# A new order for attention and two feed-forward layers on one core: one pair of blocks after the other, two batches later, sums on VectorE

## The chip, the cores and the metric

The kernel runs on one core of one Trainium2 chip. The core has TensorE (PE, matmul; its weight loads are shown apart as PEld), VectorE (DVE), ScalarE (ACT), GpSimd (POOL) and SyncE (SP), which here issues the DMA transfers. The metric is the device time of one execution in microseconds (us), as the median of the runs.

## The reference

```python
def _attn_ref(q, k, v, g_norm):            # (4 batches, 8 heads, 576, 64), float32
    kv = np.einsum('bhsd,bhse->bhde', k, v)
    out = np.einsum('bhsd,bhde->bhse', q, kv)
    rms = np.sqrt(np.mean(out * out, axis=-1, keepdims=True) + 1e-06)
    return (out / rms * g_norm).astype(np.float32)

def _moe_ref(x, w_a, w_b, w_out):          # x (2304, 512); d_ff 1536
    a = x @ w_a
    b = x @ w_b
    return (a * b @ w_out).astype(np.float32)

def _moe2_ref(x, w_in, w_out):             # d_ff 2048
    h = x @ w_in
    g = np.maximum(h, 0.0) + np.log1p(np.exp(-np.abs(h)))
    return (g @ w_out).astype(np.float32)
```

The output of the attention, heads side by side, goes through the first layer and then the second. The weights are 64-bit floats.

## The kernel before

**Numbers.** A float32 operand is split into two fp32r halves, hi (ACT) and lo (DVE: value minus hi), and a product is made of three fp32r matmuls, hi·hi, hi·lo, lo·hi. A native float32 matmul needs no split. Each weight is loaded raw (64 bits, 512 KB a tile) and turned into float32 by two ACT and one DVE operation (`w_load`, `w_start`, `w_value`), then split (`w_split`: one ACT, one DVE operation).

**Tiles.** The 2304 tokens are five blocks: four of 512 (block j is the first 512 tokens of batch j - 1), and block 0 with the 64 left of each batch. Blocks (1, 2) are pair 0, (3, 4) pair 1. For most of the work the two blocks of a pair and the two halves of the model dimension make a 2 x 2 matrix, which is multiplied in seven products instead of eight: A11, A12, A22 take blocks as they are, S1 to S4 sums of them. `x_sums` (L877) makes these sums and splits for the first layer, 14 operand tiles of 512 KB a pair; `w_sums` (L746) makes the matching sums of the weights, four DVE operations of half width for two tiles.

**Stages, as recorded.** `attention(b)` (L1311) computes a batch: kv by small matmuls, `att_o` for q times kv, the norm, the split into x. Batch 0 (NATIVE_O) copies kv (`kv_copy`) and multiplies in native float32; batches 1 to 3 split kv (`kv_half`) and q (`halves`) and use three matmuls. `slots(j)` (L1380) is the first layer for F0 = 4 of the 12 chunks of d_ff for block j of pair 0, in plain products; these chunks are fp 0 and 1 (an fp is two chunks). The other fps of pair 0 and all of pair 1 are jobs `take(n)` (L1417) in the order of ORDER: weights of the fp for both matrices, then `gated` (L909), seven products for each of a and b; for pair 1 also `first0`, block 0. A weight comes from `job_first` (L822) at first use, which also makes its sums; where the second use doesn't follow at once, it stores the float32 tiles to DRAM (`drop`), and `job_again` (L851) loads and splits them anew. `job_out` (L862) prepares w_out. After the last job of a pair `second1(pair)` (L1002) multiplies by w_out. While ORDER mixes the pairs (`x_place`, L1409), `hold` stores the 14 operand tiles of each pair to DRAM, and `take` fetches those of its pair where they are not in SBUF. `job_keep` (L757) prepares the weights of the second layer. That layer: `op_steps(pair)`, then for eight pieces a pair `stage1(i)` (L1103), seven products and softplus, and `g_sums(i)` (L1138), two sums of 128x512 on POOL, and behind the eight pieces `stage2_2(pair)` (L1162), whose operands are split from these pieces and sums; block 0 goes with pair 1 (`single1`, `single2`).

**Order and buffers.** The calls are recorded as steps (up to six matmuls into one tile are one step), and PLAN, a permutation of the steps written out by a planner, is the order in which they are emitted (`emit`, L292). Every engine and SP's queue works in that order. SBUF holds 39 big tiles of 512 KB, 28 of 256 KB, and PSUM 8 banks; a step takes a free buffer when it is emitted and waits until its last user is done. `among(main, *others)` (L1296) records the steps of others evenly between those of main. The calls around the change:

```python
    among(slots(1), attention(1))
    among(slots(2), attention(2))
    x_sums(0)
    # ...
    among(take(0), attention(3))
    x_sums(1)
```

All operations carry the line of a helper, L296, so the groups are told apart by the names of their tiles: op halves of operands, w halves of weights, w1o and w2o the output weights fetched for second1 and stage2_2, kept_* tensors in DRAM.

Of the kernel before, what the change touches and what calls it, by code (L numbers as in the profile page):

```python
# [13 lines left out]
ALU = mybir.AluOpType  # L14
# [20 lines left out]
F0 = 4  # L35
# [13 lines left out]
ORDER = ((0, 2), (1, 2), (0, 3), (0, 4), (0, 5), (1, 3), (1, 4), (1, 5), (1, 0), (1, 1))  # L49


# [4 lines left out]
NATIVE_O = (0,)  # L56
# [266 lines left out]
def attention_gated_softplus_kernel(  # L323
# [14 lines left out]
    nc = Record(tc.nc)  # L338
# [483 lines left out]
    def job_first(m, fp):  # L822
# [14 lines left out]
        for k, x in enumerate(l):  # L837
            w_load(x)
            w_start(x)
            w_value(x)  # L840
            made(k, x, 0)
        w_sums(l, True)
        for k, x in enumerate(l):
            if not plain:
                made(2 + k, x, 1)
# [712 lines left out]
```

## Time and profile before

| | us |
|---|---|
| median of 3 runs (896.19 to 897.7) | 896.82 |
| the profiled execution | 895.69 |
| its span, first to last instruction | 893.9 |
| PE busy, 4084 matmuls | 831.6 (93%) |
| PE weight loads | 676.2 (76%) |
| DVE busy, 1088 | 640.0 (72%) |
| ACT busy, 911 | 497.2 (56%) |
| POOL busy, 40 | 50.8 (6%) |
| DMA | 247.72 MB, mean 277 GB/s |

Busy time is the union of an engine's instructions, so overlapped ones count once, and a mean duration can be longer than what one more instruction costs. A wait is put down to what came last.

### The profile page before, as it was taken

The numbers are of one execution on the slowest core, as the hardware profiler recorded it, in microseconds if no ns is written. First come the engines' busy times: TensorE is split into PE (matmuls) and PEld (weight loads), VectorE is DVE, ScalarE is ACT, GpSimd is POOL, SyncE is SP. The second block draws the span as 40 slices with busy tenths as digits, with TensorE's granted clock in tenths as the row PEclk, the third lists the DMA queues.
The fourth block names the chain that finished last, engine by engine and source line by source line (L and its number), as shares of the span: only waits on it lengthen the run. The fifth ranks groups of instructions, "written<-read, shape, count | busy, mean of one in ns | idle before, by whom it ended". The sixth has DMA issues, their size and how long they took to land. (4 is left out here: it accounts for less than half of the span.)

```text
span 893.9 us, 11820 instructions
## 1 busy us (share of the span) xinstructions
PE 831.6 (93%) x4084; PEld 676.2 (76%) x4084; DVE 640.0 (72%) x1088; ACT 497.2 (56%) x911; POOL 50.8 (6%) x40
## 2 busy tenths in 40 slices
PE   7798999989989999999989999978999999988997
PEld 4576878868767887777778877757878878876785
DVE  2787999889978486888976956878763523378761
ACT  4786899867744656677646633565542211446430
POOL 0000000000000000000000000162000000090000
PEclk9998999999999999999999999998999999999999
DMA  9997799998989849988979799985679560563643
GB/s 261 324 311 272 292 320 354 401 375 324 327 280 395 328 159 334 337 299 310 334 256 385 284 408 337 327 283 177 213 244 396 182 253 22 190 209 116 195 146 124
DMA packets 109003, 247.72 MB, mean 277 GB/s; under 512 B 9616, under 2 KB 58768, under 8 KB 108944
## 3 DMA queue, kind: packets, MB, share of 16 engines
q1 hardware_dynamic: 108800, 246.98, 78.4%
q8 instruction: 32, 0.52, 0.2%
q14 instruction: 27, 0.22, 0.1%
q10 hardware_dynamic: 144, 0.00, 0.0%
HBM read 170.92 MB, written 76.02 MB: 276 GB/s over the span
## 5 line engine op out<-in xcount | busy, mean ns | idle before, releaser
L296 PE MATMUL acc<-op,w2o 128*128 128x512 f32 x672 | 161.4, 397 | 15.5 <-DVE op L296 12.1
L296 PEld LDWEIGHTS acc<-op,w2o 128*128 128x128 f32 x672 | 127.2, 191 | 46.4 <-DVE op L296 14.6
L296 DVE TENSOR_TENSOR w<-raw,w 128x512 fp32r<-128x512 f32 x168 | 113.8, 696 | 31.7 <-ACT w L296 30.8
L296 ACT ACTIVATE w<-raw 128x512 fp32r<-128x512 f32 x168 | 107.6, 669 | 48.2 <-DVE raw L296 10.3
L296 DVE TENSOR_TENSOR op<-g,op 128x512 fp32r<-128x512 f32 x156 | 110.8, 744 | 27.9 <-ACT op L296 27.7
L296 ACT ACTIVATE op<-g 128x512 fp32r<-128x512 f32 x156 | 90.9, 622 | 68.5 <-DVE g L296 36.9
L296 ACT ACTIVATE raw<-raw 128x512 int32<-128x512 uint8 (+1 forms) x136 | 88.5, 674 | 45.0 <-DMA raw<-in_w_out 30.9
L296 PE MATMUL acc<-op,w1o 128*128 128x512 f32 x420 | 100.9, 393 | 9.3 <-DMA w1o<-kept_wo 6.0
L296 PEld LDWEIGHTS acc<-op,w1o 128*128 128x128 f32 x420 | 77.2, 188 | 28.9 <-DMA w1o<-kept_wo 7.8
L296 DVE SCALAR_TENSOR_TENSOR raw<-raw 128x512 int32<-128x512 int32 x74 | 50.2, 686 | 10.3 <-ACT raw L296 10.1
L296 POOL TENSOR_TENSOR s<-g 128x512 f32<-128x512 f32 x14 | 21.2, 1520 | 581.3 <-ACT g L296 581.3
L296 PE MATMUL x<-op,w 128*128 128x512 f32 x192 | 48.5, 391 | 2.2 <-DMA w<-kept 2.2
L296 PE MATMUL v<-op,w 128*128 128x512 f32 x192 | 48.7, 391 | 0.8 <-DMA w<-kept 0.8
L296 PE MATMUL z<-op,w 128*128 128x512 f32 x192 | 48.3, 390 | 0.8 <-DMA w<-kept 0.8
L296 PEld LDWEIGHTS x<-op,w 128*128 128x128 f32 x192 | 35.6, 188 | 10.5 <-issue 1.9
L296 DVE TENSOR_TENSOR c<-z,p 128x512 f32<-128x512 f32 x32 | 21.9, 686 | 29.2 <-PE z L296 29.2
L296 PEld LDWEIGHTS z<-op,w 128*128 128x128 f32 x192 | 35.6, 188 | 8.4 <-DMA w<-kept 1.3
L296 PEld LDWEIGHTS v<-op,w 128*128 128x128 f32 x192 | 35.6, 188 | 8.4 <-DMA w<-kept 1.2
L296 PEld LDWEIGHTS h<-x,w 128*128 128x128 f32 x288 | 38.0, 191 | 5.0 <-ACT sb L296 1.5
L296 PE MATMUL h<-x,w 128*128 128x256 f32 x288 | 39.2, 283 | 1.7 <-ACT sb L296 1.1
L296 DVE TENSOR_TENSOR raw<-raw,raw 128x256 f32<-128x256 f32 x82 | 33.3, 418 | 0.4
L296 ACT ACTIVATE g<-x 128x512 f32<-128x512 f32 x16 | 9.5, 591 | 42.8 <-PE x L296 31.2
(143 smaller groups left out, 1437.3 us busy)
## 6 DMA issues: line engine op xcount, KB each, us to landing
w<-kept SPq DMA_DIRECT2D x80, 512.0 KB, 6.9
kept<-w SPq DMA_DIRECT2D x64, 512.0 KB, 6.1
w2o<-kept SPq DMA_DIRECT2D x112, 256.0 KB, 5.1
raw<-in_w_out SPq DMA_DIRECT2D x28, 512.0 KB, 6.6
w1o<-kept_ws SPq DMA_DIRECT2D x40, 256.0 KB, 6.1
kvraw<-in_kv SPq DMA_DIRECT2D x19, 448.0 KB, 9.7
kept_x_S<-op SPq DMA_DIRECT2D x16, 512.0 KB, 7.2
op<-kept_x_S SPq DMA_DIRECT2D x16, 512.0 KB, 8.4
```

The source lines that it names most:

```text
L296: f(*(x.place() if isinstance(x, View) else x for x in args), **{k: x.place() if isinstance(x, View) else x for k, x in kwargs.items()},)
```

## The change

ORDER lists the four jobs of pair 0 first and then the six of pair 1. `x_place` is then false for both pairs, so nothing is held. `attention(2)` is recorded among job 2, which is (0, 4), `attention(3)` among job 3, (0, 5). `x_sums(1)` comes behind `second1(0)`. NATIVE_O holds all four batches, with two kvf tiles in turn. The sums of the weights of fp 0 and 1 are made when they are loaded again, not at first use. `g_sums` runs on VectorE. PLAN is another permutation, of 3482 steps where there were 3534, made with transfer times taken from a trace.

```diff
-ORDER = ((0, 2), (1, 2), (0, 3), (0, 4), (0, 5), (1, 3), (1, 4), (1, 5), (1, 0), (1, 1))
+ORDER = ((0,2),(0,3),(0,4),(0,5),(1,0),(1,1),(1,2),(1,3),(1,4),(1,5))
+BATCHES_AT = {2: [2], 3: [3]}
-NATIVE_O = (0,)
+NATIVE_O = (0,1,2,3)
 PLAN = """
...
@@ job_first
-        w_sums(l, True)
+        if not plain:
+            w_sums(l, True)
@@ job_again
+        if 2 * fp < F0:
+            w_sums([(("f", m, fp, k),) for k in range(2)], True)
@@ g_sums
-        nc.gpsimd.tensor_tensor(out=t, in0=a21, in1=a22, op=ALU.add)
-        nc.gpsimd.tensor_tensor(out=a21, in0=a11, in1=a21, op=ALU.subtract)
+        nc.vector.tensor_tensor(out=t, in0=a21, in1=a22, op=ALU.add)
+        nc.vector.tensor_tensor(out=a21, in0=a11, in1=a21, op=ALU.subtract)
...
+    def run_all(steps):
+        for f in steps:
+            f()
...
     among(slots(1), attention(1))
-    among(slots(2), attention(2))
+    run_all(slots(2))
...
-    among(take(0), attention(3))
-    x_sums(1)
-    if x_place(1) or ORDER[1][0] == 0:
+    run_all(take(0))
+    if x_place(1):
+        x_sums(1)
         hold(1, True)
...
+        if n in BATCHES_AT:
+            l += [f for b in BATCHES_AT[n] for f in attention(b)]
         among(take(n), l)
         done.append(ORDER[n])
         if ORDER[n] == max(x for x in ORDER if x[0] == 0):
...
-            run(second1(0))
+            if -1 in BATCHES_AT:
+                among(drawn(second1(0), 64), [f for b in BATCHES_AT[-1] for f in attention(b)])
+            else:
+                run(second1(0))
+            x_sums(1)
```

## Rows read from the trace of the kernel before

**Rows 1.** The page: span, then busy us (share of span) and instructions of each engine.

```profile
span 893.9 us, 11820 instructions
PE 831.6 (93%) x4084; PEld 676.2 (76%) x4084; DVE 640.0 (72%) x1088; ACT 497.2 (56%) x911; POOL 50.8 (6%) x40
```

**Rows 2.** Stretches: start:end, length, busy PE, PEld, DVE, ACT, POOL (instructions), PE clock, DMA share, GB/s.

```profile
28.00:290.00 262.00, 243.20 (x1265) 195.82 (x1264) 230.55 (x421) 194.58 (x366) 0.00 (x0) 0.97 0.93 332
290.00:584.00 294.00, 279.84 (x1377) 231.59 (x1376) 222.38 (x391) 172.40 (x312) 6.89 (x5) 1.00 0.86 315
584.00:893.90 309.90, 285.47 (x1309) 234.36 (x1307) 175.38 (x252) 114.40 (x205) 42.25 (x28) 0.98 0.57 195
28.00:76.00 48.00, 39.87 (x244) 31.23 (x242) 37.16 (x70) 35.89 (x69) 0.00 (x0) 0.92 0.99 316
76.00:165.00 89.00, 88.28 (x507) 71.57 (x506) 83.34 (x153) 79.38 (x156) 0.00 (x0) 0.98 0.90 320
584.00:615.00 31.00, 22.86 (x82) 17.00 (x81) 26.49 (x29) 18.52 (x35) 18.41 (x12) 0.89 0.75 255
665.00:785.00 120.00, 118.03 (x598) 100.28 (x597) 46.51 (x73) 31.75 (x57) 2.90 (x3) 1.00 0.57 206
785.00:815.00 30.00, 25.01 (x113) 19.93 (x112) 25.57 (x27) 13.32 (x26) 20.94 (x14) 1.00 0.68 220
887.50:893.90 6.40, 0.00 (x0) 0.00 (x0) 0.65 (x1) 0.00 (x0) 0.00 (x0) 0.80 0.80 297
```

**Rows 3.** Waits of PE: tile, releaser, us in total, times, longest us.

```profile
PE acc L296 <- DVE op L296: 12.4, 7, 3.6
PE acc L296 <- DMA w1o<-kept_wo: 6.0, 3, 3.0
PE kvps L296 <- DMA kvraw<-in_kv: 4.8, 5, 2.5
PE kvps L296 <- DVE z L296: 4.7, 1, 4.7
```

**Rows 4.** Groups of POOL: tiles, shape, count, busy us, mean ns, idle before.

```profile
L296 POOL TENSOR_TENSOR g<-g,g 128x512 f32<-128x512 f32 x16 | 25.8, 1627 | 0.6
L296 POOL TENSOR_TENSOR s<-g 128x512 f32<-128x512 f32 x14 | 21.2, 1520 | 581.3 <-ACT g L296 581.3
```

**Rows 5.** Groups of DVE: two of 785 to 815 us, then two of the whole run.

```profile
L296 DVE TENSOR_TENSOR op<-g,op 128x512 fp32r<-128x512 f32 x10 | 12.1, 1237 | 0.5 <-ACT op L296 0.5
L296 DVE TENSOR_TENSOR out<-acc,out 128x512 f32<-128x512 f32 x4 | 2.7, 683 | 0.7 <-PE acc L296 0.7
...
L296 DVE TENSOR_TENSOR op<-g,op 128x512 fp32r<-128x512 f32 x156 | 110.8, 744 | 27.9 <-ACT op L296 27.7
L296 DVE TENSOR_TENSOR g<-s,g 128x512 f32<-128x512 f32 x26 | 23.2, 915 | 0.2
```

**Rows 6.** DVE in order of time: start, us, tiles, count of a run.

```profile
612.37 3.69 DVE L296 TENSOR_TENSOR op<-g,op 128x512 fp32r<-128x512 f32 x6
```

**Rows 7.** DMA issues: tiles, count, KB each, median us to landing.

```profile
kept_x_S<-op SPq DMA_DIRECT2D x16, 512.0 KB, 7.2
...
kept_x_A<-x SPq DMA_DIRECT2D x12, 512.0 KB, 6.4
```

**Rows 8.** Group of ACT, whole run: the hi halves of weights.

```profile
L296 ACT ACTIVATE w<-raw 128x512 fp32r<-128x512 f32 x168 | 107.6, 669 | 48.2 <-DVE raw L296 10.3 <-DMA kept<-w 7.9 <-DMA kept_wo<-w 6.0
```

**Rows 9.** PE in order of time; a native float32 matmul is two records.

```profile
18.49 1.12 PE L296 MATMUL ms<-sq,ones_f 128*128 128x512 f32 x2 [0.16 <-ACT sq L296]
...
44.80 0.84 PE L296 MATMUL o<-q,kvr 128*128 128x512 f32 x3
...
46.84 1.52 PE L296 MATMUL b<-x,w 128*128 128x512 f32 x6
```

**Rows 10.** Groups of PE, whole run: kv products, and mean squares of batches 1 to 3.

```profile
L296 PE MATMUL kvps<-kvraw 112*64 112x64 f32 x256 | 14.8, 271 | 0.4 <-DMA kvraw<-in_kv 0.4
...
L296 PE MATMUL ms<-s,ones 128*128 128x512 f32 x24 | 8.5, 423 | 0.6 <-DVE s L296 0.6
```

More of the change, by code (lines that the diff above doesn't have):

```diff
@@ L1294, in run @@
                 pass
+    def run_all(steps):
+        for f in steps:
+            f()
     def among(main, *others):
-        main, beside = list(main), [f for x in others for f in x]
+        main = list(main)
+        beside = [f for x in others for f in ([x] if callable(x) else x)]
         n = 0
```

285 rows, old and new, of the table PLAN are left out of this document.

## The prediction

> **What bounds the kernel now.** I began with the page's busy shares: TensorE (PE) works 831.6 of 893.9 us, VectorE (DVE) 640 and ScalarE (ACT) 497 [rows 1]. PE is the bound, so a change is worth the PE idle that it closes, the slow-clock time that it gives back, and the PE work that it adds. Next I read the table of busy time by stretch [rows 2]. From 28 us (batch 0 is through) to 290 us (end of the first pair's output products) PE is busy 243.2 of 262 us, so 18.8 us are idle; from 290 to 584 us 279.8 of 294 (14.2 idle); from 584 us on 285.5 of 309.9, of which 6.4 us are the last stores, which stay (18.0 idle without them). That makes 51.0 us of idle that an order could close. The granted clock is below full in few places: 0.97 of 2.4 GHz over the first stretch, 0.92 from 28 to 76 us, 0.89 from 584 to 615 us, each where PE had stood idle just before; times the lengths that is 7.9 us lacking in the first stretch, 3.8 of it before 76 us, and 3.4 us from 584 to 615 us.
>
> Then the table of who waited for whom, PE's lines [rows 3]: 12.4 us in seven waits for DVE's halves of the operands (op), 6.0 us for w1o tiles from DRAM, 4.8 us for the k and v loads, 4.7 us in one wait for a DVE result z. The reader is to see two clots in the stretches: 584 to 615 us (8.1 us idle) and 785 to 815 us (5.0 us). Both are the start of a stage2_2, both are where GpSimd (POOL) works, 18.4 and 20.9 us, and DVE is busy 26.5 of 31 and 25.6 of 30 us [rows 2]. The other thing to see is DMA: share 0.93 from 28 to 290 us at 332 GB/s, that is nearly full, 0.86 and then 0.57 behind it.
>
> **The sums of g, from POOL to DVE.** 16 pieces with two sums each are 32 operations, of 1.5 to 1.6 us on POOL [rows 4]. While POOL works, DVE operations with two operands in SBUF are slower: the lo halves of the operands take 1.237 us in 785 to 815 us, additions with one operand in PSUM (out<-acc,out) keep 0.683 us there [rows 5]. Over the whole run the 156 lo halves have a mean of 0.744 us and the 26 subtractions g<-s,g of 0.915 us, so against 0.683 us POOL costs DVE 156 x 0.061 + 26 x 0.232 = 15.5 us. On DVE, six such operations in a row take 3.69 us [rows 6], so one costs (3.69 - 0.68) / 5 = 0.60 us once the pipeline runs; 32 are 19.3 us. DVE's net load rises by 4 us. What changes is where it lies: a sum can run as soon as its piece has left stage1, and there DVE has room, 46.5 of 120 us busy from 665 to 785 us [rows 2]. So the two clots should go in great part: 13.1 us idle and 3.4 us of clock are the most (-16.5), and nothing gained with the 4 us of net load put into the same two stretches (+4) is the other end. I take -9.5 (8 of idle, 1.5 of clock), nearer the gain, since the slowed operations are the very ones (op) that PE waits for [rows 3, 5].
>
> The Trainium skill, SBUF — State Buffer, section Who interferes with whom, says that a DVE instruction with two SBUF inputs and a GpSimd instruction that reads SBUF exclude each other, and whoever comes second is blocked for the whole instruction of the first. The trace agrees on which forms are hit; by the rule at its strictest the 47 us of the two large POOL groups [rows 4] would all be lost to such DVE instructions and this term would be the full -16.5, while the rows show a loss of 15.5 us of DVE time, and I keep to them.
>
> **Pair 0 first, then pair 1: no parking.** ORDER held pair 1's (1, 2) between pair 0's jobs, so the 14 operand tiles of either pair were stored to DRAM and fetched again: 16 + 12 stores of 512 KB, for which two rows stand; the two rows of the fetches have the same counts [rows 7]. In the new ORDER each pair is one run, x_place is false for both, and all 56 go. Against that fp 2's weights are no longer used twice in a row: four more stores (drop) and four more loads (job_again). Net 48 transfers, 25.2 MB, at 332 GB/s [rows 2] 76 us of full queue, out of a stretch of 262 us whose DMA share is 0.93. SP issues in order, so 56 instructions that can wait for a buffer or an operand also go from ahead of weight loads. What of it reaches PE: the part of the w1o wait (6.0) and of the k/v wait (4.8) that lies here, and waits that stand behind late weights [rows 3]. Bounds: 0 (every transfer hidden, the waits come from issue order) and -18.8 (all idle of the stretch). I take -6, about half of the 10.8 us of waits for transfers. The four more job_again splits of each engine pair, 8 on ACT (0.64 us, 107.6 / 168 [rows 8]) and 8 on DVE (0.60), are 5 us each; they lie beside PE's second half of the pair-1 jobs, where DVE was busy 222.4 of 294 us [rows 2]; without that cover, +5.
>
> **Batches 2 and 3 later.** attention(2) leaves slots(2) for the job (0, 4), attention(3) leaves take(0) for (0, 5). x_sums(1) moves behind second1(0). For fps 0 and 1 the 16 half-wide w_sums leave the start and are done on refetch. In 28 to 76 us PE has 8.1 us idle and 3.8 us of clock lacking at a DMA share of 0.99 [rows 2]; without batch 2's loads (3.5 MB) and the w_sums I take -4 (3 idle, 1 clock); bounds -11.9 and +5 (another wait like the 4.7 us one for z [rows 3] appears). What is late next there is the weights' conversion on ACT and DVE.
> The price is a bulge later. DVE in one of the two jobs: by the code 22 full and 8 half-wide operations for the job itself (4 values, 8 splits, 10 on its products; 8 sums), 6 and 4 for job_out, 20 and 5 for the attention batch. 48 x 0.60 + 17 x 0.35 (half-wide, an estimate by scale) = 34.8 us. PE in the same job: six matmuls take 1.52 us, three 0.84 [rows 9], so (1.52 - 0.84) / 3 = 0.227 each and 19.0 us for 84; and of attention 80 short ones (14.8 / 256 each, 4.6 us), 8 of ms (8.5 / 24 each, 2.8 us) [rows 10] and 4 native o of about 1.0 us: 11.4, together 30.4 us. DVE lags by 4.4 us per job, 8.8 for both, unless weights are prepared earlier; up to 165 us the old order ran DVE at 83.3 of 89 us with PE at 88.3 [rows 2], so such a load can be carried. Bounds 0 and +8.8; I take +4.
> x_sums(1) now stands just ahead of pair 1's first job. A11 needs no sum, and the first S1 needs an addition and a split, 2 us of DVE, under the 2.7 us of the two A11 products (12 x 0.227). Cost 0; +2 without this cover.
>
> **kv·q in native fp32 for all batches.** Gone: the q halves, 5 on ACT and 5 on DVE for each of three batches, and kv_half (4 a batch); new: 8 small copies a batch. That frees some 8 us on each engine, hidden now as then, worth 0 by itself but part of why the bulge is taken at +4. On PE three fp32r products of 0.84 us merged become one native product; the nearest row is batch 0's native one with the same shape, 1.12 us at the full clock [rows 9]. 12 x 0.28 = +3.4 us; the 64-column tails shrink from 12 matmuls to 4 native ones, -0.4 us each by estimate (12 short ones against 8 half-products of about the same step). I take +2; bounds -1 (tails gain, rest hidden in idle) and +3.4.
> The Trainium skill, FP8 and Floating Point Precision, section TensorE Precision Notes, counts four passes for true fp32; against the three here that speaks against this part of the change. By it the term would be 12 x 0.227 = +2.7 us before the tails; no run here separates the passes.
>
> **The new plan as such.** PLAN is a new permutation of 3482 steps (3534 before), made with the transfer times of a trace. Nothing in the trace prices it. From 290 to 584 us, where the work stays nearly the same, 14.2 us are idle [rows 2]. I take -3; bounds +7 (half as much again) and -14.2.
>
> **Sum.** -9.5 - 6 - 4 + 4 + 2 - 3 = -16.5 us. Span 893.9 - 16.5 = 877.4. The profiled execution took 895.69 us, 1.8 more than its span, and the median of the runs is 896.82, 1.1 more than that: 877.4 + 2.9 = 880.3, so 880 us.
>
> **Rivals.**
> A, most gaps close: transfer times were what the old plan lacked, two thirds of the 51.0 us of idle go (-34), 5 us of clock come back, +2 stays: -37, 860 us. For it: no engine but PE is full after 290 us, and from 665 to 785 us PE was already busy 118 of 120 [rows 2]. Against: from 76 to 165 us DVE was about as full as PE.
> B, nothing moves: transfers were hidden anyway, PE waits at other operands as DMA and POOL go off the path, the sums bring -7 of their -9.5, and the attention bulge (+4) and native (+2) take all of it but 1. 896 us. For it: PE's own waits for transfers are only 10.8 us [rows 3].
> C, slower: DVE becomes the bound from the first pair's jobs to second1(0), because the four jobs of pair 0 with all four job_outs and two batches no longer have (1, 2) with its shared weights among them. It decides from the point at which DVE can't be held above 90% there. By the counts above, job (0, 3) has 16.0 us for itself and 5.0 for a job_out: 21.0 / 0.9 - 19.0 = 4.3 us; (0, 4) and (0, 5) 34.8 / 0.9 - 30.4 = 8.3 each; the last job_out stands alone, 5.0: 25.9. If a third of that is made ahead, +17; the start gives nothing, the plan nothing, the sums -9.5, parking -6, native +2, fp 2's refetch uncovered +5: +8.5, 905 us. For it: in 76 to 165 us both engines were full [rows 2]. Against: q halves are gone from DVE.
>
> **Chances.** Forecast 0.50 (866 to 893), A 0.22, B 0.11, C 0.17. The range takes in most of A and reaches to 900, below most of C and above B: 856 to 900. About 0.2%, 1.8 us, is what a measurement of this kernel can tell from no change: faster 0.73, same 0.11, slower 0.16 (a few of C's cases end within it).
>
> **What would show it.** Sums: no POOL work after 2 us, DVE's op at 0.68 us throughout, PE idle at the two starts of stage2_2 under 5 us together and the clock there at 1.00. Parking: no kept_x rows, DMA traffic near 222.5 MB, share before 290 us clearly under 0.9. Bulge: DVE at 95% while PE is under 90% in a stretch of some 60 us before the first pair's output products; that would be C. Native: o<-qr,kvf at 1.1 us in all batches. The prediction is wrong if the idle at the starts stays (then operand halves on ACT were the limit, not POOL) or if a new wait of over 5 us stands between second1(0) and pair 1.

## The result and the profile after

The changed kernel takes 824.77 us (median of four runs, 824.59 to 825.12) against 896.57 us (896.19 to 897.7): a ratio of 0.9198, 95% interval 0.9182 to 0.9214, so 72 us less. The forecast was 880 us, with a range of 856 to 900: the sign was right, and the gain was four times the one forecast and outside the range.

The page of the changed kernel, with the lines that answer to [rows 1]; then its DMA line and its chain that ended last:

```profile
span 823.3 us, 11636 instructions
PE 804.6 (98%) x4060; PEld 666.7 (81%) x4060; DVE 635.1 (77%) x1120; ACT 497.8 (60%) x911; POOL 1.7 (0%) x8
DMA packets 102091, 222.55 MB, mean 270 GB/s; under 512 B 8848, under 2 KB 58000, under 8 KB 102032
PE 94%; ACT 3%; DVE 1%; DMA 1%; SPq 0%; issue 0%
```

Busy time by stretch, which answers to [rows 2] (start:end, length, busy PE, PEld, DVE, ACT, POOL, granted clock, DMA share, GB/s):

```profile
0.00:28.00 28.00, 17.03 (x127) 11.32 (x127) 8.61 (x21) 12.97 (x22) 0.70 (x7) 0.94 0.98 246
28.00:100.00 72.00, 70.76 (x367) 54.89 (x366) 64.65 (x119) 67.06 (x128) 0.00 (x0) 1.00 0.94 331
100.00:250.00 150.00, 150.00 (x807) 120.99 (x806) 147.34 (x271) 121.47 (x232) 0.00 (x0) 1.00 0.87 293
250.00:400.00 150.00, 150.00 (x774) 128.71 (x773) 131.79 (x243) 103.38 (x186) 0.00 (x0) 1.00 0.75 267
400.00:550.00 150.00, 150.00 (x731) 126.97 (x730) 125.89 (x219) 91.49 (x166) 0.00 (x0) 1.00 0.94 347
550.00:700.00 150.00, 150.00 (x739) 127.28 (x738) 78.65 (x128) 52.59 (x95) 0.96 (x1) 1.00 0.65 224
700.00:817.00 117.00, 116.60 (x528) 96.58 (x526) 77.33 (x125) 48.85 (x85) 0.00 (x0) 1.00 0.54 176
```

And all of PE's waits, which answer to [rows 3] (tile, releaser, us in total, times, longest us):

```profile
PE kvps L296 <- DMA kvraw<-in_kv: 9.1, 1, 9.1
PE o L296 <- ACT kvf L296: 1.9, 1, 1.9
PE a L296 <- DVE z L296: 0.8, 1, 0.8
PE a L296 <- ACT w L296: 0.4, 1, 0.4
PE acc L296 <- ACT c L296: 0.4, 1, 0.4
```

From 32 us on PE stands still for under 1 us in all until the last stores. What is left is the wait for the first kv load, two small waits of batch 0, and 6 us of stores at the end. The span fell by 70.6 us; PE's idle time fell from 62.3 to 18.7 us (43.6) and its busy time from 831.6 to 804.6 us (27.0). The second number is the surprise, since PE's work is almost the same. The same 672 matmuls of stage2_2, first in the kernel before and then in the changed one (count, busy us, mean ns, idle before and what ended it):

```profile
L296 PE MATMUL acc<-op,w2o 128*128 128x512 f32 x672 | 161.4, 397 | 15.5 <-DVE op L296 12.1 <-DMA w2o<-kept 2.9 <-ACT op L296 0.5
```

```profile
L296 PE MATMUL acc<-op,w2o 128*128 128x512 f32 x672 | 155.3, 390 | 0.4 <-ACT c L296 0.4
```

At 0.227 us each, the step from start to next start in a full stretch, they are 152.5 us of work. Where PE stopped often, 8.9 us more were counted as busy: each stop leaves a matmul's whole shown length standing (0.390 us in the mean of the second line), where in a full stretch the next one starts 0.227 us later; and the granted clock was low there (0.89 from 584 to 615 us [rows 2]). Where it doesn't stop, 2.8 us more are left. So a stop costs more than the idle time that the wait table shows for it. The mean granted clock rose from 0.985 to 0.997; (1 - 0.985) x 893.9 = 13.4 us were lacking before and 2.5 us are lacking now, at most 10.9 us of the 27.

### The profile page after: what moved, and what is told of

Its sections match the earlier page's. It is cut to its first block, busy times and chain, and to the rows that moved or that the text cites. A ratio compares the mean times of both kernels' runs of the same rounds, so it can differ in the third digit from the quotient of the medians.

```text
span 823.3 us, 11636 instructions
## 1 busy us (share of the span) xinstructions
PE 804.6 (98%) x4060; PEld 666.7 (81%) x4060; DVE 635.1 (77%) x1120; ACT 497.8 (60%) x911; POOL 1.7 (0%) x8
## 2 busy tenths in 40 slices
DMA packets 102091, 222.55 MB, mean 270 GB/s; under 512 B 8848, under 2 KB 58000, under 8 KB 102032
## 4 chain that ended last, share of the span: by engine, by line
PE 94%; ACT 3%; DVE 1%; DMA 1%; SPq 0%; issue 0%
PE acc L296 37%; PE h L296 7%; PE x L296 5%; PE z L296 5%; PE v L296 5%; PE xa L296 3%; PE xb L296 3%; PE za L296 3%; PE yb L296 3%; PE zb L296 3%; PE ya L296 3%; PE y L296 3%; PE a L296 2%; PE b L296 2%; PE o L296 2%; PE va L296 2%
## 5 line engine op out<-in xcount | busy, mean ns | idle before, releaser
L296 PE MATMUL acc<-op,w2o 128*128 128x512 f32 x672 | 155.3, 390 | 0.4 <-ACT c L296 0.4
L296 PEld LDWEIGHTS acc<-op,w2o 128*128 128x128 f32 x672 | 125.5, 188 | 26.4 <-ACT c L296 0.8
L296 ACT ACTIVATE w<-raw 128x512 fp32r<-128x512 f32 x176 | 114.2, 670 | 37.7 <-DVE raw L296 16.6
L296 DVE TENSOR_TENSOR w<-raw,w 128x512 fp32r<-128x512 f32 x176 | 117.1, 685 | 18.4 <-ACT w L296 17.9
L296 ACT ACTIVATE op<-g 128x512 fp32r<-128x512 f32 x156 | 93.2, 625 | 48.7 <-PE acc L296 29.0
L296 DVE TENSOR_TENSOR op<-g,op 128x512 fp32r<-128x512 f32 x156 | 102.6, 684 | 17.3 <-ACT op L296 16.3
L296 PE MATMUL acc<-op,w1o 128*128 128x512 f32 x420 | 99.1, 391 | 0.0
L296 ACT ACTIVATE raw<-raw 128x512 f32<-128x512 f32 (+1 forms) x136 | 88.0, 674 | 10.6 <-DMA raw<-in_w_out 8.6
L296 ACT ACTIVATE g<-c 128x512 f32<-128x512 f32 x32 | 19.4, 624 | 36.6 <-DVE c L296 19.0
L296 PE MATMUL yb<-op,w 128*128 128x512 f32 x120 | 31.5, 397 | 0.0
```

Source lines behind the costliest of these rows:

```text
L296: f(*(x.place() if isinstance(x, View) else x for x in args), **{k: x.place() if isinstance(x, View) else x for k, x in kwargs.items()},)
```

## The experiments

All ratios are set against runs of the kernel before on the same chip, whose medians are 892.98 to 897.02 us and whose single runs 889.25 to 902.56 us. Differences of a few us between two experiments can be of the chip. Where an order is called "searched", the permutation of the kernel's own steps was searched for by local moves, with durations and landing times read from the traces of the two kernels; the work is untouched. Of PLAN each diff shows the start of its first row.

### The order alone: old_work_new_order

```diff
 PLAN = """
-18 14 15 5 7 2 3 4 12 38 17 23 16 19 20 28 1 93 41 22 21 39 40 24 2
+18 2 3 1 4 12 14 8 15 38 23 16 13 9 19 17 28 5 20 41 21 6 22 39 40
...
```

> The old kernel's work unchanged (parking, sums on GpSimd, q halves, batches 2 and 3 early in the record); only PLAN is another permutation, searched for by local moves with the durations and landing times read from the two traces. Theory O (the order alone makes the gain): 825 to 845 us, PE idle under 30 us in all, clock at 0.99 or above. Theory W (the removed work makes it: parked tiles, GpSimd's sums): 870 us or more, with PE idle left at the two starts of stage2_2 and a DMA share over 0.9 before 290 us.

Measured: 851.98 us, ratio 0.9522 (0.949 to 0.9554): -43 us of the 72, with parking, GpSimd's sums, early batches and split q all in place. That lies between the two theories, nearer to that of the order. PE's idle time fell from 62.3 to 32.3 us and its busy time from 831.6 to 817.4 us. From its page, and then the longest of PE's waits that are left:

```profile
span 849.7 us, 11989 instructions
PE 817.4 (96%) x4084; PEld 669.9 (79%) x4084; DVE 642.6 (76%) x1088; ACT 505.5 (59%) x912; POOL 49.1 (6%) x40
```

```profile
PE acc L291 <- DVE op L291: 5.5, 8, 2.2
PE z L291 <- DVE p L291: 3.4, 2, 2.1
PE za L291 <- DMA op<-kept_x_A: 3.3, 2, 3.1
```

Of all the waits listed for PE, those that a transfer ended fell from 22.0 us (21 waits) to 6.6 (6), those that DVE ended from 25.1 to 16.4, those that ACT ended from 8.9 to 5.1. The larger part of the gain is the order as such, the term that the prediction held at -3.

### The sums alone: old_vector_sums

```diff
-        nc.gpsimd.tensor_tensor(out=t, in0=a21, in1=a22, op=ALU.add)
-        nc.gpsimd.tensor_tensor(out=a21, in0=a11, in1=a21, op=ALU.subtract)
+        nc.vector.tensor_tensor(out=t, in0=a21, in1=a22, op=ALU.add)
+        nc.vector.tensor_tensor(out=a21, in0=a11, in1=a21, op=ALU.subtract)
```

> The old kernel with its old order; only the two sums of each piece run on VectorE instead of GpSimd, at the same places of the order. The prediction's term: 887 us (-9.5), with at most 5 us of PE idle left from 584 to 615 and 785 to 815 us. Theory O: the old order has its waits elsewhere too and these sums wait in VectorE's own queue: 885 to 897 us. Theory W: 880 us or less.

Measured: 886.82 us, ratio 0.9926 (0.9887 to 0.9965): -8 us by the medians, 3 to 10 by the interval (ten runs, 883.74 to 895.65 us); the span of the profiled execution is 10.9 us shorter. The two clots open, but in part: PE was busy 22.86 and 25.01 us in these stretches [rows 2], and is now as the next two lines show. 8.1 and 5.0 us of idle have become 5.7 and 1.9; the 7.6 us together are above the 5 us of the prediction's sign, and the clock of the first is 0.94, not 1.00. PE's wait for the halves (last line) was 12.4 us [rows 3]:

```profile
584.00:615.00 31.00, 25.28 (x100) 19.30 (x99) 29.59 (x49) 21.75 (x40) 0.00 (x0) 0.94 0.68 227
785.00:815.00 30.00, 28.14 (x126) 22.78 (x125) 26.91 (x45) 19.31 (x35) 0.00 (x0) 1.00 0.63 203
```

```profile
PE acc L291 <- DVE op L291: 6.4, 4, 2.9
```

### The sums back on GpSimd in the new order: new_gpsimd_sums

```diff
-        nc.vector.tensor_tensor(out=t, in0=a21, in1=a22, op=ALU.add)
-        nc.vector.tensor_tensor(out=a21, in0=a11, in1=a21, op=ALU.subtract)
+        nc.gpsimd.tensor_tensor(out=t, in0=a21, in1=a22, op=ALU.add)
+        nc.gpsimd.tensor_tensor(out=a21, in0=a11, in1=a21, op=ALU.subtract)
```

> The new kernel with its new order; only the two sums of each piece run on GpSimd as before. The prediction's term: 834 us (+9.5). Theory O: the new order leaves slack around the pieces, so 826 to 832 us. Theory W: 838 us or more.

Measured: 826.86 us, ratio 0.9236 (0.9206 to 0.9267), 2.1 us above the changed kernel; the intervals of the two ratios just overlap, so the difference is hardly clear of noise. DVE is slowed as it was in the kernel before (0.744 us [rows 5]), but PE hardly sees it; first DVE's lo halves, then PE's wait for them:

```profile
L292 DVE TENSOR_TENSOR op<-g,op 128x512 fp32r<-128x512 f32 x156 | 111.4, 743 | 19.1 <-ACT op L292 19.1
```

```profile
PE acc L292 <- DVE op L292: 0.7, 2, 0.4
```

12.4 us of that wait [rows 3] have become 0.7 with the same slow operations. A slower DVE costs next to nothing here, where its results are early enough.

### Loads later in the new order: new_late_loads

372 of the changed kernel's 412 loads are emitted later, to some 4 us before their first use; nothing else is moved.

```diff
 PLAN = """
-17 39 15 2 42 19 16 20 18 24 94 29 53 8 3 4 5 21 22 1 108 34 64 13
+2 15 19 16 20 8 3 4 5 17 39 42 18 24 94 21 22 1 13 23 95 25 26 40 2
...
```

> The new kernel with all its work; only the places of 372 loads from DRAM in PLAN are later, so that each is issued about 4 us before its first use (or where it stood, if that was later). Theory O in the form that the lead of the loads is what the old order lacked: 850 to 880 us, with PE waiting for w, w1o and w2o. If the lead was not it: 825 to 835 us. Theory W: 825 to 830 us.

Measured: 868.37 us, ratio 0.971 (0.9671 to 0.9749): 43.6 us of the 72 are lost again. The changed work with late loads is only 27 us under the kernel before, and 27.5 of the 37.8 us of PE's listed waits are for loads, most of them in these two lines:

```profile
PE kvps L291 <- DMA kvraw<-in_kv: 13.0, 5, 5.6
PE y L291 <- DMA w<-kept: 11.4, 2, 9.5
```

### Loads earlier in the old order: old_early_loads

428 loads of the kernel before are emitted up to 5 us earlier, where a buffer is free for them.

```diff
 PLAN = """
-18 14 15 5 7 2 3 4 12 38 17 23 16 19 20 28 1 93 41 22 21 39 40 24 2
+33 52 41 93 28 16 23 17 38 15 14 18 5 7 2 3 4 12 19 20 1 63 111 22
...
```

> The old kernel with its old order, only 428 loads from DRAM are emitted earlier, by up to 5 us of the old trace, as far as a buffer is free at that place. If the lead of the loads alone was what the old order lacked: 870 to 888 us. If the buffers set it (a load that takes a buffer early makes the next user of that buffer, and all behind it on its engine, wait): slower than before, 905 us or more.

Measured: 1025.28 us (two runs), ratio 1.1476 (1.1361 to 1.1591), 132 us slower. The packets of the DMA queue take 69.8% of the engines' span, where they took 78.4%, and PE waits 146 us in all, longest for DVE's halves (16.5 us), weights (13.1) and kv (10.7). ACT shows waits for buffers: its hi halves of weights now wait 55.6 us for the stores of earlier weight tiles, where it was 7.9 [rows 8]; by the code a step waits until the last user of its buffer is done.

```profile
L291 ACT ACTIVATE w<-raw 128x512 fp32r<-128x512 f32 x168 | 108.9, 669 | 116.7 <-DMA kept<-w 55.6
```

So a load that comes early can hold a buffer that something else needed first, and "earlier" alone isn't what the new order does. That the new order gains by its choice of which tiles hold the buffers fits this, but no run shows it by itself.

### Both at once in the old work: old_vector_new_order and old_vector_longer_search

The kernel before with its sums on DVE (the diff of old_vector_sums) and the order searched; in the second run searched further.

```diff
 PLAN = """
-18 14 15 5 7 2 3 4 12 38 17 23 16 19 20 28 1 93 41 22 21 39 40 24 2
+18 2 3 1 4 12 6 15 13 14 5 19 38 20 21 7 17 16 22 39 40 44 23 24 25
...
```

> The old kernel's work, with the sums on VectorE, in an order searched for in the same way as in old_work_new_order (852.0 us, where PE and VectorE stalled while GpSimd worked: 7.6 us of PE idle from 550 to 600 us). Theory P (of the 27 us that old_work_new_order lacks, GpSimd's sums are the larger part, since that search knew nothing of what they do to VectorE): 832 to 840 us. Theory W (the rest is parking and the early batches): 846 to 852 us.

Measured: 838.09 us, ratio 0.9382 (0.9327 to 0.9438), 13.9 us under old_work_new_order. The order was searched anew with the sums on DVE, so these 13.9 us are of the sums and of another order together.

> The work of old_vector_new_order (the kernel before with its sums of g on DVE, parking kept, batches 2 and 3 where they were, native product for batch 0 only), its order searched on from the one that took 838.1 us. Theory P (the order of this work is about used up, the 13.3 us to the changed kernel are in its work): 833 to 839 us. Theory Q (the order alone holds the rest): 829 us or less.

Measured: 838.49 us, ratio 0.9372 (0.9305 to 0.9439): no better. This search finds nothing more in the old work, 13.7 us above the changed kernel.

### The same search on the changed work: new_work_new_order

```diff
 PLAN = """
-17 39 15 2 42 19 16 20 18 24 94 29 53 8 3 4 5 21 22 1 108 34 64 13
+2 3 4 13 5 15 14 19 16 1 20 6 39 18 21 24 17 7 22 42 94 23 29 40 53
...
```

> The new kernel's work in an order found by the same search, started from the new PLAN. It tells what the search is worth on the new work, so that the old work's result can be set beside it. If the new PLAN leaves only the start and the last stores (some 39 us above the sum of PE's steps, 784 us): 818 to 826 us. If more of the start can be closed: 805 to 817 us.

Measured: 824.81 us, ratio 0.923 (0.9165 to 0.9295), the time of the changed kernel. Its order is as good as any found here, and no version beat it.

### The native product in the old work: old_vector_native_new_order

```diff
-NATIVE_O = (0,)
+NATIVE_O = (0,1,2,3)
```

> As old_vector_longer_search, but with the native float32 product in all four batches, order searched for the same way. Theory N (a native product takes PE 0.45 to 0.56 us against 3 x 0.227 = 0.68, the sum of PE's steps falls by 3.8 us): 3 to 5 us under old_vector_longer_search. Theory F (a native product costs PE more than the three split ones, as the prediction had it, +2 to +3.4): 2 us or more above it. ACT's and DVE's freed 8 us each may add to N and not to F.

Measured: 842.21 us (839.17 to 846.6) against 838.49 (834.82 to 843.75): the median is 3.7 us higher, the way of theory F, but the runs overlap, so the time alone decides nothing. The records do. In PE's order of time (start, us shown, tiles, records), the changed kernel has

```profile
42.88 1.12 PE L296 MATMUL o<-qr,kvf 128*128 128x512 f32 x2
43.44 1.26 PE L296 MATMUL a<-x,w 128*128 128x512 f32 x3
44.54 1.52 PE L296 MATMUL acc<-ghl,w 128*128 128x512 f32 x6
...
54.95 1.02 PE L296 MATMUL o<-qr,kvf 128*128 128x512 f32 x2
55.40 1.26 PE L296 MATMUL acc<-ghl,w 128*128 128x512 f32 x3
56.50 0.85 PE L296 MATMUL b<-x,w 128*128 128x512 f32 x3
```

and the kernel before, for a split product (its first row stands in [rows 9]),

```profile
45.48 0.84 PE L296 MATMUL a<-x,w 128*128 128x512 f32 x3
46.16 0.84 PE L296 MATMUL o<-q,kvr 128*128 128x512 f32 x3
46.84 1.52 PE L296 MATMUL b<-x,w 128*128 128x512 f32 x6
```

From start to next start, a split product takes 0.68 us (7 of the 12 in the kernel before take 0.680). A native one seems to take 0.455 us (8 of the 16 in the changed kernel take 0.455 to 0.456), but that isn't its cost: the matmul behind it is late. The three fp32r matmuls from 55.40 to 56.50 us take 1.10 us where three take 0.68, since the first of them takes 0.63 us to the next start and not 0.227. From 54.95 to 56.50 us the native product and these three take 1.55 us, so the native product 0.87 us; where one native product follows another, each of its two records takes 0.429 us, 0.858 us a product. That is 0.18 us more than a split one, 2.1 us for the twelve of three batches. The tails go the other way: eight records of a batch's four native tails take 0.81 us where the twelve split ones take 1.256 (one after the other at 150.13 us), and the matmul behind either is late by the same 0.09 us, which is 0.45 us a batch and 1.3 us for three. By PE's steps the native products cost the changed kernel 0.8 us.

### Parking's traffic put into the changed kernel: new_parking, new_parking_new_order, new_parking_narrow

28 operand tiles are stored to DRAM and copied there once more; nobody reads them. In new_parking these transfers are issued between 28 and 363 us, 50 of the 56 from 110 us on, in new_parking_new_order between 167 and 824 us. In new_parking and new_parking_narrow the transfers are laid into the changed kernel's order at fixed places, in new_parking_new_order the whole order is searched again with them in it.

```diff
+    for n, x in enumerate(again):
+        to, back = (kept.tile([P, 2, 512], F32, name=f"again_{k}_{n}") for k in "ab")
+        nc.sync.dma_start(out=to, in_=x.bitcast(F32))
+        nc.sync.dma_start(out=back, in_=to)
```

> The new kernel with the traffic of parking put back beside its work: each of the 28 operand tiles of x_sums is stored to DRAM once more, and copied once more from DRAM to DRAM in place of the fetch (56 transfers of 512 KB, from 112 to 330 us, on SP's queue); nobody waits for them. The prediction's term: 831 us (+6). Theory O (an order with slack hides it): 825 to 829 us. Theory W (parking filled the queue, so that weights came late): 840 us or more, with PE waiting from 115 to 330 us.

Measured: 849.17 us, ratio 0.9514 (0.9454 to 0.9573), 24.4 us above the changed kernel.

> new_parking (the changed kernel with 28 extra stores of 512 KB and 28 copies of 512 KB within DRAM, which nobody reads), which took 849.2 us with the transfers laid in at fixed times; here the whole order is searched for again with them in it. Theory H (the transfers hide once the order makes room for them): 824 to 831 us. Theory X (29.4 MB more in that stretch cost PE time in any order): 836 us or more, most of the 24.4 us.

Measured: 847.57 us, ratio 0.9476 (0.9412 to 0.9539). With the whole order free, 22.8 us stay: the order found doesn't hide the traffic. From 400 to 550 us PE, busy 150.00 us there in the changed kernel, stands beside a full queue:

```profile
400.00:550.00 150.00, 142.10 (x681) 116.82 (x680) 115.96 (x201) 83.28 (x149) 0.00 (x0) 1.00 1.00 363
```

In new_parking_narrow the same transfers at the same places move 32 columns of 512:

```diff
-        nc.sync.dma_start(out=to, in_=x.bitcast(F32))
-        nc.sync.dma_start(out=back, in_=to)
+        nc.sync.dma_start(out=to[:, :, 0:32], in_=x.bitcast(F32)[:, :, 0:32])
+        nc.sync.dma_start(out=back[:, :, 0:32], in_=to[:, :, 0:32])
```

> new_parking (the changed kernel with 28 stores and 28 copies within DRAM that nobody reads, 849.2 us) with the same 56 transfers at the same places of SP's queue, waiting for the same operands, but of 32 columns in place of 512 (32 KB each, 1.8 MB in all in place of 29.4). Theory T (the traffic costs: the transfers fill the DMA engines and other loads land later): 824 to 830 us. Theory Q (the issues cost: SP's queue stands behind a store that waits for its operand, or is busy with 56 more issues): 840 us or more.

Measured: 838.88 us, ratio 0.9358 (0.9302 to 0.9415): between the two theories. 14.1 us stay with a sixteenth of the bytes, 10.3 us go with the traffic. Most of the 14.1 us have one place. SP's waits from 55 to 110 us, then the first row of its issues behind the longest one (the queue had issued nothing from 60 us on), then the stretches (columns as above):

```profile
SPq L294 <- DVE x L294: 17.3, 2, 16.8
```

```profile
75.51 1.61 SPq L294 DMA_DIRECT2D again_a<-x  x2
```

```profile
65.00:75.00 10.00, 10.00 (x49) 8.37 (x48) 9.54 (x18) 9.03 (x18) 0.00 (x0) 1.00 0.01 2
75.00:85.00 10.00, 5.65 (x26) 4.51 (x24) 3.67 (x6) 1.40 (x3) 0.00 (x0) 0.88 0.71 211
85.00:95.00 10.00, 6.64 (x20) 5.28 (x21) 4.91 (x9) 7.62 (x15) 0.00 (x0) 0.61 1.03 419
```

A store stood at the head of SP's queue for 16.8 us until its operand was written. No load behind it was issued, the DMA engines emptied (share 0.01), and from 75 us on ACT, DVE and PE ran dry (1.40, 3.67 and 5.65 of 10 us); PE waited 7.7 us in one piece, and the clock went to 0.61 behind it: 7.7 us of idle and 5.1 of clock from 75 to 95 us, where PE is busy throughout in the changed kernel. new_parking has the same store (SP waits 16.8 us, PE 8.1 us in one piece). So the 24.4 us of new_parking aren't a price of traffic alone: by this run some 10 are, and 14 are a badly placed store. In the kernel before no store of an operand tile stood so long: SP waited for op 14.1 us in 15 pieces, the longest 4.3, and for x 4.3 us in four.

## Why the prediction was wrong, step by step

**What bounds the kernel.** PE is the bound, as said, before and after. The step that failed is the use of its busy time as a floor. 51.0 us of reducible idle were taken as all that an order could close; 43.6 us of idle closed, and 27.0 us of busy time with them. That busy time held the lengths shown of matmuls at a stop and the slow clock; the prediction set 11.3 us of lacking clock beside it and took back 2.5. Adding each step of PE at its usual start-to-next-start time (0.227 us for 128x512, 0.120 for 128x256, 0.429 for each record of a native 128x512) gives, by estimate, about 792 us for the kernel before and 0.8 more for the changed one: without the last stores the room was some 95 us, nearly twice what was reckoned. The Trainium skill, Perfetto Trace Analysis, section Tensor Engine Instruction (MATMUL, LD_WEIGHTS), says that the end shown for a matmul is estimated and not observed; the 0.390 us shown against a step of 0.227 us agree.

**The new plan as such, -3 with bounds +7 and -14.2.** This is the term that was mis-sized: -43 by old_work_new_order, with the old work. Its bounds were the idle time of one stretch, 290 to 584 us, but the new order is one of the whole kernel: with the old work it closed 30.0 us of idle and 14.2 of busy time. A second misreading lies beside it: the 10.8 us of "PE's own waits for transfers" are two of the four lines of [rows 3], and all lines that a transfer ended are 22.0 us in 21 waits, of which 6.6 are left in old_work_new_order. Why the new orders are better stays open. One explanation is the lead of the loads, the time from a load's landing to its first use, taken from the records of each: in the kernel before 92 of 436 loads were first used within 1 us of landing, in the changed one 23 of 412; the raw tiles of the second layer's w_in had landed 0.52 us before their first use in the median, and 7.32 us in the changed kernel. The other runs speak against it. In old_work_new_order, 43 us faster than the kernel before, 82 of 436 loads are used within 1 us and the w_in tiles 0.30 us after landing; in old_vector_longer_search, at 838 us, it is 89, and in old_early_loads, at 1025 us, only 44. new_late_loads shows that taking the lead away costs time (+43.6, 71 of 412 loads within 1 us), not that lead is what the old order lacked.

**The sums, -9.5.** Right in size for the old order: -8 us by the medians, though only 5.5 of the 8 us of idle closed at the two places named. In the changed kernel POOL is gone (POOL 1.7 us, lo halves 0.684 us). As a share of this change it is no fixed number: up to -13.9 with an order searched for the old work, -2.1 in the changed kernel's. The Trainium skill, SBUF — State Buffer, section Who interferes with whom, says that the second comer is blocked for the whole instruction of the first, and the prediction weighed this as a loss of all of POOL's time. The records agree with the blocking and not with that loss: in the kernel before 11 of the 156 lo halves meet a sum on POOL and take 0.87 to 1.78 us, the others at most 0.70 us. The rows of new_gpsimd_sums show the same slowing (0.743 us in the mean) and PE hardly waiting: what is lost is DVE's time, and what that costs depends on the slack behind it.

**Parking, -6 with bounds 0 and -18.8.** Both parts of the mechanism, the issues in SP's queue and its fullness, can cost time, as the added traffic shows. The size in this change isn't settled: traffic of this size put into the changed kernel costs some 10 us by itself in fixed places and 22.8 in the order searched for it, but a copy within DRAM isn't a load, and the old work carries its own parking in a searched order at 13.7 us above the changed kernel. From 28 to 290 us the DMA share went from 0.93 [rows 2] to 0.81; 222.55 MB are as forecast.

**Batches and bulge, -4 and +4.** The bulge is there: DVE 147.34 of 150 us from 100 to 250 us. It costs nothing, PE is at 150.00. Rival C, with DVE as the bound, had its place right and its point of decision wrong: DVE can be held above 98%. At the start, PE is busy 17.03 us in the first 28, with one wait of 9.1 us for kv, and then 70.76 of 72 up to 100 us. Added up at PE's usual steps, the changed kernel has done 81.1 us of work by 100 us and the kernel before 72.0, but old_work_new_order, with the early batches in place, has done 80.9: this gain needs no later batches.

**Native, +2.** Right in sign by PE's steps, and within the bounds: +0.8 us. The price of a product was too high, 0.28 us where the steps show 0.18, because 1.12 us against 0.84 are lengths shown and each holds one modelled end; the tails give back 0.45 us a batch, as estimated (0.4). The Trainium skill, FP8 and Floating Point Precision, section TensorE Precision Notes, counts four passes for true fp32; the rows agree, with 0.858 us a native product, four times 0.2145, against 0.227 us for one fp32r matmul.

**The rivals.** A (most gaps close, 860 us) named the right term, the plan, and was held back by the same ceiling: it closed 34 us of idle and gave back 5 of clock, and let the rest of the busy time stand. Two thirds of the room of some 95 us would have been 63 us, or about 835 us. Whether transfer times were what the old plan lacked, as A has it, isn't shown: the searches used durations as well, and the lead of the loads doesn't explain the gain.

**What stays open.** A searched order brings 43 us in the old work, and the sums with an order searched for them 14 more; the last 13.7 us are no parking, later batches, the moved sums of weights and the native products together. Native costs 0.8 us of PE's steps and frees ACT and DVE, and shows no gain in time where it was tried alone; the batches weren't tried alone. What the new orders do better than the old one isn't found. The parts don't add up independently of the order, so a single price for each can't be given. And the searched orders are those of one search: that a better one exists for the old work isn't excluded.

## What to carry to other kernels

Where one engine is the bound, add up its steps from start to next start in full stretches before using its busy time as a floor: stops hide in busy time. Take such a step over a whole sequence and not from one record: part of a native product's time lies in the step of the matmul behind it. Where an order is planned by hand or by a program, try another order of the same work before pricing the rest: here one took 43 us off 895. The count of loads that land just in time didn't foretell it (82 of 436 after, 92 before). A change that only moves waits off other engines (a slow sum, a bulge) is worth what the slack behind it lacks (8 us for the sums in the old order, 2 in the new), so price it in the new order, not in the old.

## What was not expected of the hardware

A native float32 product of 128x512 lets the next matmul start 0.455 us after its own start, and then that matmul takes 0.63 us in place of 0.227: the product costs 0.86 us, more than three fp32r ones (0.680 us). And one store waiting at the head of SP's queue for 16.8 us empties all 16 DMA engines (share 0.01 for 10 us) and costs the kernel some 14 us, 7.7 of them one wait of PE.
